# Two linear-attention and MLP layers on one core: x loads, the order of a key's split, deferred queries' phi, and the plan of the first MLP block

## The chip, the core and the metric

The kernel runs on one core of a Trainium2 chip. The metric is the device time of one execution in microseconds (us). Engines are named as in the profile: PE is the matrix engine (TensorE), DVE is VectorE, ACT is ScalarE, POOL is GpSimd, SP is the engine whose queue issues all DMAs here. Each engine takes its instructions strictly in the order in which the kernel writes them.

## The reference

x is 2048 x 448 in fp32. A layer of linear attention (16 heads of 28) and an MLP (448 to 1792 to 448) are applied twice, with the same weights:

```python
def _A_ref(x, wqkv, wo):
    q, k, v = ...                                   # (x @ wqkv), 16 heads
    phi = lambda t: jnp.where(t > 0, t + 1, jnp.exp(t)) + 1e-6
    pq, pk = phi(q), phi(k)
    kv = jnp.einsum("bhsd,bhse->bhde", pk, v)
    z = jnp.einsum("bhsd->bhd", pk)
    num = jnp.einsum("bhqd,bhde->bhqe", pq, kv)
    den = jnp.einsum("bhqd,bhd->bhq", pq, z)[..., None] + 1e-6
    return (num / den) @ wo                          # heads joined again
def _B_ref(x, w1, b1, w2, b2):
    return gelu(x @ w1 + b1) @ w2 + b2               # tanh form
x = x + _A_ref(_layernorm(x), A_wqkv, A_wo)
x = x + _B_ref(_layernorm(x), B_w1, B_b1, B_w2, B_b2)
x = x + _A_ref(_layernorm(x), A_wqkv, A_wo)
x = x + _B_ref(_layernorm(x), B_w1, B_b1, B_w2, B_b2)
```

## The kernel before

x is cut into 16 tiles of 128 rows; four tiles make a block. fp32 products are made of three matmuls on rounded halves: a value is split into hi (a copy in the format fp32r) and lo (the value minus hi), and hi·hi, hi·lo and lo·hi are added up. Most work off PE is this splitting: ACT writes hi, DVE or POOL subtracts for lo.

A layer has three stages.

**Phase 1** (`phase1`, L474) takes a tile per step t. Tokens of a string say what a step writes, in order (`STEP` L458; the first step of each layer has its own, `STEP_0` L459): `a` statistics of the tiles that `NORM[l][t]` names (one or two, ahead of t; `ln_stats` L179: bn_stats, bn_aggr, an add on DVE, a pow on POOL), `n` their normalisation (L359 on DVE; for early tiles a copy of the last 64 columns, `tail` L363, on ACT), `T` and `X` the transposed x of tile t+1 split into XH and XL (for the first tiles of layer 0 on PE into a PSUM bank, L232; later tiles by DVE's 32x32 transposes, `tu`/`tv` L255, a store to DRAM L261 and a load that spreads it, L267, token `sp`), `K` the product for k (psk), `kp` its phi (two ACT passes L293 and L294, one DVE instruction L296), `kh` its split into kh (ACT, L411) and kl (DVE, L412) and the running sum za, `s` the split of x into xnh (ACT) and xnl (POOL), `G` the sum over the previous tile of x times phi(k) in four PSUM banks, `Q` the product for q (psq) and `qp` its phi, stored to pq_d in DRAM (L430); `bg` brings in and splits pieces of w1 and w2. v is never made: G is multiplied by v's weights afterwards. Loads of x (`load_x` L80, nine buffers) are asked for at the start of each step up to one tile past the ones that the next step normalises (L480).

PSUM has eight banks: tag "m" has two (k, and later transposes), "h" two (q, transposed x in layer 0, later the MLP's hidden hp), "acc" four. Work buffers have tags too; "e" has three and holds phi's intermediate results and later the MLP's g.

**Between the phases**, `ORDER` (L450) writes out by hand what happens for the first block: `Q` and `Qp` for the last queries, deferred from phase 1, `z` and `gt` (z and G copied to SBUF), `kv`, `mask`, `m`/`ms` (the combined matrix M and its split), `qz`/`qs` (the denominator's product on POOL and `q_scale` L616 on DVE), `tq`/`qq` (q transposed and split), `o` (q times M), `la` (added to x, statistics), `lb` (`o_n` L675: normalisation, and the last 64 columns a second time by L196, then b2 added to x by POOL, L678), `T`/`x` (transposed and split for the MLP).

**The MLP** takes four blocks of four tiles. For each of its 14 slices of the hidden width, `mlp1` (L705) makes hp, ACT's GELU g (L717), gh (L720) and gl (DVE, L721); `mlp2` (L724) adds g times w2 into four banks y, and the last slice adds y to x on DVE (L735) and stores it. Behind the slices of a block, `behind` (L786) prepares the next one, step by step, by a plan: `PLAN_0` (L743) for block 0, `PLAN_1` and `PLAN` after. Its tokens: `ld` load pq, `z` and `p` the denominator, q_scale and DVE's transposes of a later block's queries, `sq`/`lq` store and spread them, `q`, `o`, `n` as above, `sx`/`lx` store and spread the normalised x, `x` split it, `g` load x. From step 7 on `z`, `p`, `sq` and `lq` serve the block after next.

Of the kernel before, what the change touches and what calls it, by code (L numbers as in the profile page):

```python
# [22 lines left out]
def linear_attn_mlp_kernel(  # L23
# [47 lines left out]
    def t512(tag, bufs, name, dt=F32):  # L71
        return work.tile([128, 512], dt, name=name, tag=tag, bufs=bufs)
# [114 lines left out]
        pool.tensor_tensor(rs, ve, mhalf, op=OP.pow)  # L187
        return xs, mv, rs

    def ln_norm(stats, name, twice=True):  # L190

        xs, mv, rs = stats
        xn = t512("xn", 2, name)
        dve.tensor_scalar(xn[:, :D], xs, mv[:, 0:1], rs, op0=OP.subtract, op1=OP.mult)  # L194
        if twice:
            dve.tensor_scalar(xn[:, D:], xs[:, TL:], mv[:, 0:1], rs, op0=OP.subtract, op1=OP.mult)  # L196
        return xn


# [25 lines left out]

    tps = {}

    def transpose_x(xn, key, j, tail=None, tag="m"):
        block(key)
        tp = tps[key, j] = bank(tag, 2, "tp")  # L230
        for c in range(4):
            pe.transpose(tp[:, c * 128:(c + 1) * 128],  # L232
                         tail if tail is not None and c == 3 else xn[:, c * 128:(c + 1) * 128], ident)

    def split_x(key, j):
        tp = tps.pop((key, j))
# [138 lines left out]

    def stage_b(l, t):
        if t < TURNED[l]:
            transpose_x(xns[l, t], ("a", l, t // 4), t % 4, tails.pop((l, t)), "h")

    def stage_x(l, t):  # L380
        key = ("a", l, t // 4)
# [22 lines left out]

    ke = {}

    def stage_kh(l, t, za):
        e = ke.pop((l, t))
        kh = t512("E", 2, "kh", F32R)[:, :D]
        kl = t512("F", 2, "kl", F32R)[:, :D]  # L410
        act.activation(kh, e, AF.Identity, bias=tiny)  # L411
        dve.scalar_tensor_tensor(kl, e, 1e-6, f(kh), op0=OP.add, op1=OP.subtract)  # L412
        if t == 0:
            dve.tensor_copy(za, e)
        else:
            dve.tensor_tensor(za, e, za, op=OP.add)
        ks[l, t] = (kh, kl)
# [3 lines left out]
    def stage_q(l, t):  # L421
        if t is None:
            return
        qo.append((l, t, proj("q", ("a", l, t // 4), t % 4)))

    def stage_qphi():
        while qo:
            l, t, o = qo.pop(0)
            e = phi(o, "eq")
            sp.dma_start(pq_d[l][t * 128:(t + 1) * 128, :], e)  # L430

    def stage_g(l, t, acc):
        h, lo = split.pop((l, t))
        kh, kl = ks.pop((l, t))
        first, last = t == 0, t == NT - 1
        for c in range(3):
            s = slice(c * 128, (c + 1) * 128)
            pe.matmul(acc[c], h[:, s], kh, start=first, stop=False)  # L438
            pe.matmul(acc[c], h[:, s], kl, start=False, stop=False)  # L439
            pe.matmul(acc[c], lo[:, s], kh, start=False, stop=last)  # L440
        pe.matmul(acc[3], h[:, TL:], kh, start=first, stop=False)
        pe.matmul(acc[3], h[:, TL:], kl, start=False, stop=last)
# [5 lines left out]


    ORDER = (  # L450
# [4 lines left out]
    )  # L455
    DEFER = NT - ORDER.split().count("Q")

    STEP = "a qp K T X s n G kp tu kh tv bg Q sp"  # L458
    STEP_0 = "K T X w a kp n s kh tu tv G Q bg sp", "K T X s kp a kh n tu tv G Q bg sp"  # L459
    NORM = (  # L460
        ((2,), (3, 4), (5, 6), (7,), (8,), (9,), (10, 11), (12,), (13, 14), (15,)),
        ((5,), (6,), (7,), (8,), (9, 10), (11,), (12,), (13, 14), (15,)),
# [11 lines left out]
    def phase1(l, tr):  # L474
        za = consts.tile([128, D], F32, name="za", tag="za")
        acc = [bank("acc", 4, f"G{c}")[:, :D] for c in range(4)]
        for t in range(NT):
            norm = NORM[l][t] if t < len(NORM[l]) else ()
            if t + 1 < len(NORM[l]):
                load_to(l, min(NORM[l][t + 1][-1] + 1, NT - 1))  # L480
            for tok in (STEP if t else STEP_0[l]).split():
                if tok == "sp":
                    for u in norm:
                        if u % 2:
                            stage_sp(l, u)
                elif tok == "a":
                    for u in norm:
                        stage_a(l, u)
                elif tok == "n":
                    for u in norm:  # L490
                        stage_n(l, u)
                elif tok == "tu":
                    for u in norm[:1]:
                        stage_t(l, u)
                elif tok == "tv":
                    for u in norm[1:]:
                        stage_t(l, u)
                elif tok == "w":
                    split_hi("q", 3, st_q)
                    split_lo("q", 3, st_q, dve)  # L500
                elif tok == "T" and t + 1 < NT:
                    stage_b(l, t + 1)
                elif tok == "X" and t + 1 < NT and (l == 0 or t + 1 >= 4):
                    stage_x(l, t + 1)
                elif tok == "K":
                    stage_k(l, t)
                elif tok == "qp":
                    stage_qphi()
                elif tok == "kp":
                    stage_kphi(l, t)  # L510
                elif tok == "kh":
                    stage_kh(l, t, za)
                elif tok == "s":
                    stage_s(l, t)
                elif tok == "G" and t >= 1:
                    stage_g(l, t - 1, acc)
                elif tok == "bg" and l == 0:
                    background(BG[t])
                elif tok == "Q" and t < DEFER:
                    stage_q(l, t)  # L520
            if l == 0 and t == 4:
                sp.dma_start(b1s, b1.rearrange("(c p) -> p c", p=128))
                sp.dma_start(b2b, b2[None, :].to_broadcast([128, D]))
            if t == 11:
                tr.wv = stage_square(wqkv[:, 2 * D:])
            if t == 13:
                trans_load(l, tr)
        return za, acc
# [19 lines left out]
    def trans_gt(tr, acc):  # L548
        tr.gt = []
        for c in range(4):  # L550
            s = t512("A" if c < 2 else "B", 2, "gt")[:, :D]
            if c % 2 == 0:
                act.copy(s, acc[c])
            else:
                dve.tensor_copy(s, acc[c])
            tr.gt.append(s)

    def trans_kv(tr):
# [115 lines left out]

    def o_n(l, b, j):  # L675
        t = b * 4 + j
        xns["m", l, t] = ln_norm(sts.pop(("m", l, t)), f"xm{l}_{t}", b == 0)
        pool.tensor_tensor(xt[l, t], xt[l, t], b2b, op=OP.add)  # L678

    def m_transpose(l, b, j):  # L680
        transpose_x(xns.pop(("m", l, b * 4 + j)), ("m", l, b), j)

    def m_split(l, b, j):
        split_x(("m", l, b), j)
# [39 lines left out]
    def mlp2(l, b, i, acc):  # L724
# [23 lines left out]
        "q0 lq1",  # L748
        "q1 o0",
        "o1 n0 q2 ld0",  # L750
        "o2 n1 sx0 q3",
        "o3 n2 lx0 ld1",
        "n3 sx1 ld2",
        "x0 lx1 ld3 z0",
        "x1 p0 z1",
        "x2 x3 p1 sq0 z2",
        "p2 z3 lq0",
    )
    LATER = (
        "n3 sx1 ld1 ld2",  # L760
# [82 lines left out]
    for l in range(LAYERS):  # L843
# [6 lines left out]
        def pre(j):  # L850
# [2 lines left out]
            q_z(l, 1, 0, tr)  # L853

        tok_ = SimpleNamespace(
            Q=lambda j: stage_q(l, fill.pop(0)), Qp=lambda j: stage_qphi(), G=lambda j: stage_g(l, NT - 1, acc),
            ld=lambda j: (load_pq(l, 0, j), load_x(l, j)), z=lambda j: trans_z(tr, za), gt=lambda j: trans_gt(tr, acc),
            kv=lambda j: trans_kv(tr), mask=lambda j: trans_mask(tr), m=lambda j: trans_m(tr, j),
            ms=lambda j: trans_ms(tr, j), qz=lambda j: q_z(l, 0, j, tr), qs=lambda j: q_scale(l, 0, j, tr),
# [10 lines left out]
        for b in range(NB):  # L870
            acc = [bank("acc", 4, f"y{j}")[:, :D] for j in range(4)]
            nxt = b + 1 < NB
            if not nxt and l + 1 < LAYERS:
                st_k = stage_square(wqkv[:, D:2 * D])
                st_q = stage_square(wqkv[:, :D])
                load_to(l + 1, PRE - 1)
            for i in range(NF):
                if i + 1 < NF:
                    mlp1(l, b, i + 1)
                elif nxt:  # L880
                    mlp1(l, b + 1, 0)
                if l == 0 and b == 0:
                    background(1 if i else 2, 0 if not i else 1)
                if nxt:
                    behind(l, b, i, tr)
                elif l + 1 < LAYERS:
                    if i == 2:
                        split_kq("k", st_k)
                    if i == 5:
                        split_kq("q", st_q)  # L890
                    if i in (3, 4, 6, 7, 8):
                        t = (3, 4, 6, 7, 8).index(i)
                        stage_a(l + 1, t)
                        stage_n(l + 1, t)
                        stage_t(l + 1, t)
                        if t % 2:
                            stage_sp(l + 1, t)
                    if 9 <= i < 13:
                        stage_x(l + 1, i - 9)
                mlp2(l, b, i, acc)  # L900
# [28 lines left out]
```

## Time and profile before

| | us |
|---|---|
| median of three runs | 896.62 (896.31 to 897.45) |
| the profiled execution, its own time | 895.62 |
| its span, first to last instruction | 893.9 |

| engine and what it waited for | idle time before that group of instructions, us |
|---|---|
| DVE, for gh (L721) | 307.3 |
| ACT, for hp (L717) | 403.4 |
| POOL, for the sum before the pow (L187) | 304.8 |

PE's granted clock is at full speed in all 40 slices of the page; DMA engines are busy 5 to 7 tenths of the time in the first eighth of the span, and mostly 1 to 5 later. A line of a timeline has: start, duration, engine, line of the kernel, operation, what it writes <- what it reads, how many, and in brackets the idle time before and what ended it. "SPq" is SP's queue of DMA issues, with the time that SP spent on them, not the transfer. Matmuls overlap their neighbours, so a matmul of 0.36 us is followed by the next after 0.20 us.

In layer 0, phase 1 runs from 6.9 to about 115 us, the work between the phases until 147.8 us, when the first hp matmul starts. Layer 1's phase 1 has its first G matmul at 460.02 us.

### The profile page before, as it was taken

To read this page: it belongs to the slowest core of one execution; us is meant where nothing else is said; L and a number is where in the kernel's file an instruction comes from. 1 tells how busy PE (TensorE), PEld (TensorE's weight loads), DVE (VectorE), ACT (ScalarE), POOL (GpSimd) and SP (SyncE) were. 2 spreads that over 40 slices of the span, in tenths; PEclk is the share of its full clock that TensorE was granted. 3 is DMA by queue.
4 is the path that set the end of the run, shared out by engine and by line. 5 is a ranking of instruction groups with operands and counts; after the bars stand their busy time and mean duration, and the time that the engine had idled before them with its cause. 6 is when DMAs were issued, how large, how long until landed. Compare 5 with 4: busy or idle time off the path is not lost.

```text
span 893.9 us, 11662 instructions
## 1 busy us (share of the span) xinstructions
PE 879.7 (98%) x4190; PEld 771.8 (86%) x4190; DVE 498.3 (56%) x968; ACT 338.3 (38%) x582; POOL 209.1 (23%) x241
## 2 busy tenths in 40 slices
PE   8999999999999999999999999999999999999998
PEld 6898978888788888888889998888878888888887
DVE  6787686655754544225469866864565473532112
ACT  5666744333222322333345564343132233223221
POOL 4566723422112012002023332320311210210000
PEclk9999999999999999999999999999999999999999
DMA  5486622723513412051145542053233323111001
GB/s 164 138 231 217 200 85 89 224 64 102 171 51 91 141 36 77 18 176 48 47 138 178 181 122 94 21 178 113 71 103 129 97 86 130 37 59 37 4 1 42
DMA packets 62761, 93.70 MB, mean 105 GB/s; under 512 B 8816, under 2 KB 57968, under 8 KB 62704
## 3 DMA queue, kind: packets, MB, share of 16 engines
q1 hardware_dynamic: 62704, 92.97, 32.9%
q8 instruction: 33, 0.54, 0.3%
q14 instruction: 24, 0.20, 0.1%
HBM read 55.65 MB, written 34.08 MB: 100 GB/s over the span
## 4 chain that ended last, share of the span: by engine, by line
PE 85%; DVE 8%; ACT 2%; DMA 2%; issue 2%; SPq 1%; POOL 1%; DVEq 0%; POOLq 0%
PE y L729 10%; PE y L731 10%; PE y L730 10%; PE hp L713 9%; PE hp L712 9%; PE hp L711 9%; PE hp L715 3%; PE hp L714 3%; PE G L439 2%; PE op L664 2%; PE op L663 2%; PE op L665 2%; PE G L440 2%; PE G L438 2%; PE psk L283 2%
## 5 line engine op out<-in xcount | busy, mean ns | idle before, releaser
L721 DVE TENSOR_TENSOR gl<-g,gh 128x512 fp32r<-128x512 f32 x112 | 79.5, 710 | 307.3 <-ACT gh L720 307.3
L717 ACT ACTIVATE g<-hp,b1s 128x512 f32<-128x512 f32 x112 | 77.1, 688 | 403.4 <-PE hp L715 403.2
L729 PE MATMUL y<-w2h,gh 128*128 128x448 f32 x448 | 163.8, 366 | 1.7 <-ACT g L717 1.7
L731 PE MATMUL y<-w2h,gl 128*128 128x448 f32 x448 | 163.7, 365 | 0.0
L730 PE MATMUL y<-w2l,gh 128*128 128x448 f32 x448 | 163.6, 365 | 0.0
L713 PE MATMUL hp<-XL,w1h 128*128 128x512 f32 x336 | 131.3, 391 | 0.3 <-DVE XL L274 0.3
L711 PE MATMUL hp<-XH,w1h 128*128 128x512 f32 x336 | 131.5, 391 | 0.1
L712 PE MATMUL hp<-XH,w1l 128*128 128x512 f32 x336 | 131.6, 392 | 0.0
L187 POOL TENSOR_TENSOR brs<-bve,mhalf 128x1 f32<-128x1 f32 x64 | 39.7, 620 | 304.8 <-DVE bve L185 302.0
L729 PEld LDWEIGHTS y<-w2h,gh 128*128 128x128 f32 x448 | 84.1, 188 | 11.4 <-ACT g L717 2.5
L730 PEld LDWEIGHTS y<-w2l,gh 128*128 128x128 f32 x448 | 84.1, 188 | 8.3
L731 PEld LDWEIGHTS y<-w2h,gl 128*128 128x128 f32 x448 | 84.2, 188 | 6.7
L713 PEld LDWEIGHTS hp<-XL,w1h 128*128 128x128 f32 x336 | 63.1, 188 | 14.8 <-DVE XL L274 1.2
L711 PEld LDWEIGHTS hp<-XH,w1h 128*128 128x128 f32 x336 | 63.1, 188 | 11.7 <-ACT XH L273 0.8
L712 PEld LDWEIGHTS hp<-XH,w1l 128*128 128x128 f32 x336 | 63.1, 188 | 11.2
L720 ACT CAST gh<-g 128x512 fp32r<-128x512 f32 x112 | 69.7, 622 | 3.6
L614 POOL TENSOR_TENSOR pz<-pq,zb 128x448 f32<-128x448 f32 x32 | 36.7, 1149 | 105.3 <-DVE dn L620 74.4
L392 POOL TENSOR_TENSOR xnl<-x,xnh 128x384 fp32r<-128x384 f32 x32 | 37.4, 1168 | 45.2 <-ACT xnh L391 20.4
L181 DVE BATCH_NORM_STATS2 bst<-x 128x6 f32<-128x448 f32 x64 | 39.7, 621 | 10.0 <-DMA x<-in_A_x_dram 7.4
L678 POOL TENSOR_TENSOR x<-x,b2b 128x448 f32<-128x448 f32 x32 | 36.9, 1152 | 31.5 <-DVE xm L194 23.3
L715 PE MATMUL hp<-XL,w1x 128*128 128x512 f32 x112 | 43.6, 389 | 0.0
L714 PE MATMUL hp<-XH,w1x 128*128 128x512 f32 x112 | 43.6, 389 | 0.0
(140 smaller groups left out, 1571.4 us busy)
## 6 DMA issues: line engine op xcount, KB each, us to landing
x<-in_A_x_dram SPq DMA_DIRECT2D x32, 224.0 KB, 4.2
pq_d<-eq SPq DMA_DIRECT2D x32, 224.0 KB, 2.1
pq<-pq_d SPq DMA_DIRECT2D x32, 224.0 KB, 3.3
x<-x_d SPq DMA_DIRECT2D x32, 224.0 KB, 3.6
sq_a<-sq SPq DMA_DIRECT2D x13, 512.0 KB, 2.6
sp<-sq_a SPq DMA_DIRECT2D x52, 128.0 KB, 3.0
sq_q<-sq SPq DMA_DIRECT2D x12, 512.0 KB, 2.8
sp<-sq_q SPq DMA_DIRECT2D x48, 128.0 KB, 3.0
```

The lines of the kernel that those rows point to most:

```text
L181: dve.bn_stats(st, xs)
L711: pe.matmul(o, w1h[:, c, s], x.moving(x.hi, c), start=(c == 0), stop=False)
L712: pe.matmul(o, w1l[:, c, s], x.moving(x.hi, c), start=False, stop=False)
L713: pe.matmul(o, w1h[:, c, s], x.moving(x.lo, c), start=False, stop=False)
L714: pe.matmul(o, w1x[:, s], x.moving(x.hi, 3), start=False, stop=False)
L715: pe.matmul(o, w1x[:, s], x.moving(x.lo, 3), start=False, stop=True)
L717: act.activation(g, hp, AF.Gelu_apprx_tanh, bias=b1s[:, i:i + 1])
L720: act.copy(gh, g)
L721: dve.tensor_sub(gl, g, f(gh))
L729: pe.matmul(acc[j], gh[:, s], w2h[:, i], start=first, stop=False)
L730: pe.matmul(acc[j], gh[:, s], w2l[:, i], start=False, stop=False)
L731: pe.matmul(acc[j], gl[:, s], w2h[:, i], start=False, stop=last)
```

## The change

- `stage_kh` is cut in two: `stage_kh` (ACT) and `stage_kl` (DVE, za). In `STEP_0` kh is written ahead of the next tile's norm and split (layer 0) and kl has a place of its own; layer 1's first step has `n` ahead of `kl`. A new `STEP_1` serves steps 1 to 3 of layer 0, with `qp`, `K`, `T`, `X` ahead of `a`.
- Loads of x are asked for at the end of a step (`ld`, ahead of `sp`), up to the tiles that the step after next normalises.
- The six deferred queries get `fill_qphi`: exp and both relus on ACT, the add on POOL, two "e" buffers, one query for each `Qp`; `ORDER` is rewritten, with the third `Q` ahead of `tq0`.
- gt's four copies are all on ACT; the second copy of xm's last columns moves from DVE (L196) to ACT; the adds of b2 move out of `o_n` into the first four steps of each MLP block (`add_bias`).
- In `PLAN_0` p0, p1 and p2 of the block after next come one or two steps earlier, and x2 and x3 one step earlier; the last step is empty.

```diff
-    def stage_kh(l, t, za):
+    def stage_kh(l, t):
+        kh = t512("E", 2, "kh", F32R)[:, :D]
+        act.activation(kh, ke[l, t], AF.Identity, bias=tiny)
+        ks[l, t] = (kh,)
+
+    def stage_kl(l, t, za):
         e = ke.pop((l, t))
-        kh = t512("E", 2, "kh", F32R)[:, :D]
+        kh, = ks[l, t]
         kl = t512("F", 2, "kl", F32R)[:, :D]
-        act.activation(kh, e, AF.Identity, bias=tiny)
         dve.scalar_tensor_tensor(kl, e, 1e-6, f(kh), op0=OP.add, op1=OP.subtract)
...
+    def fill_qphi():
+
+        l, t, o = qo.pop(0)
+        e = t512("e", 3, "eq")[:, :D]
+        p = t512("e", 3, "ep")[:, :D]
+        act.activation(e, o, AF.Relu, scale=-1.0)
+        act.activation(e, e, AF.Exp, scale=-1.0)
+        act.activation(p, o, AF.Relu)
+        pool.tensor_tensor(e, p, e, op=OP.add)
+        sp.dma_start(pq_d[l][t * 128:(t + 1) * 128, :], e)
...
     ORDER = (
-        "Q ld1 z ld0 ld2 qz0 qz1 G gt qs1 Qp Q kv qs0 tq1 mask qz2 tq0 qs2 ld3 "
-        "m0 qq1 m1 qz3 ms0 qs3 m2 ms2 m3 ms1 qq0 ms3 Q tq2 Qp o0 la0 tq3 qq2 qq3 "
-        "lb0 o1 o2 la1 T0 la2 o3 Q lb1 lb2 x0 la3 Qp T1 x1 T2 Q lb3 Qp x2 "
-        "T3 x3 Q Qp pre "
+        "Q ld1 z ld0 ld2 qz0 qz1 G gt qs1 Q Qp kv qs0 tq1 Q mask qz2 tq0 qs2 ld3 "
+        "m0 qq1 Qp m1 qz3 ms0 qq0 m2 ms1 m3 ms2 tq2 ms3 qs3 o0 Qp la0 tq3 qq2 qq3 "
+        "o1 lb0 o2 la1 T0 la2 o3 Q lb1 x0 lb2 T1 la3 T2 x1 Q Qp lb3 x2 "
+        "T3 x3 Q Qp Qp pre "
     )
-    STEP = "a qp K T X s n G kp tu kh tv bg Q sp"
-    STEP_0 = "K T X w a kp n s kh tu tv G Q bg sp", "K T X s kp a kh n tu tv G Q bg sp"
+    STEP = "a qp K T X s n G kp kh tu kl tv bg Q ld sp"
+    STEP_0 = "K T X w a kp kh n kl s Q bg ld sp", "K T X s kp a kh n kl tu Q ld sp"
+    STEP_1 = "qp K T X a s n G kp kh tu kl tv bg Q ld sp"
...
-            if t + 1 < len(NORM[l]):
-                load_to(l, min(NORM[l][t + 1][-1] + 1, NT - 1))
-            for tok in (STEP if t else STEP_0[l]).split():
+            if t == 0:
+                load_to(l, NORM[l][1][-1])
+            for tok in (STEP_0[l] if t == 0 else STEP_1 if l == 0 and t < 4 else STEP).split():
...
+                elif tok == "ld" and t + 2 < len(NORM[l]):
+                    load_to(l, NORM[l][t + 2][-1])
...
-            if c % 2 == 0:
-                act.copy(s, acc[c])
-            else:
-                dve.tensor_copy(s, acc[c])
+            act.copy(s, acc[c])
...
     def o_n(l, b, j):
         t = b * 4 + j
-        xns["m", l, t] = ln_norm(sts.pop(("m", l, t)), f"xm{l}_{t}", b == 0)
+        xn = xns["m", l, t] = ln_norm(sts.pop(("m", l, t)), f"xm{l}_{t}")
+        if b == 0:
+            act.copy(xn[:, D:], xn[:, TL:D])
+
+    def add_bias(l, b, j):
+        t = b * 4 + j
         pool.tensor_tensor(xt[l, t], xt[l, t], b2b, op=OP.add)
...
-        "o2 n1 sx0 q3",
-        "o3 n2 lx0 ld1",
-        "n3 sx1 ld2",
-        "x0 lx1 ld3 z0",
-        "x1 p0 z1",
-        "x2 x3 p1 sq0 z2",
+        "o2 n1 sx0 q3 ld1",
+        "o3 n2 lx0 ld2 z0",
+        "n3 sx1 ld3 p0 z1",
+        "x0 lx1 p1 z2 sq0",
+        "x1 x2 x3",
         "p2 z3 lq0",
+        "",
```

More of the change, by code (lines that the diff above doesn't have):

```diff
@@ L188, in ln_stats, with ln_norm @@
         return xs, mv, rs
-    def ln_norm(stats, name, twice=True):
+    def ln_norm(stats, name):
         xs, mv, rs = stats
@@ L194, in ln_norm @@
         dve.tensor_scalar(xn[:, :D], xs, mv[:, 0:1], rs, op0=OP.subtract, op1=OP.mult)
-        if twice:
-            dve.tensor_scalar(xn[:, D:], xs[:, TL:], mv[:, 0:1], rs, op0=OP.subtract, op1=OP.mult)
         return xn
@@ L226, in linear_attn_mlp_kernel, with transpose_x @@
     tps = {}
-    def transpose_x(xn, key, j, tail=None, tag="m"):
+    def transpose_x(xn, tail, key, j, tag="m"):
         block(key)
@@ L231, in transpose_x @@
         for c in range(4):
-            pe.transpose(tp[:, c * 128:(c + 1) * 128],
-                         tail if tail is not None and c == 3 else xn[:, c * 128:(c + 1) * 128], ident)
+            pe.transpose(tp[:, c * 128:(c + 1) * 128], xn[:, c * 128:(c + 1) * 128] if c < 3 else tail, ident)
     def split_x(key, j):
@@ L377, in stage_b @@
         if t < TURNED[l]:
-            transpose_x(xns[l, t], ("a", l, t // 4), t % 4, tails.pop((l, t)), "h")
+            transpose_x(xns[l, t], tails.pop((l, t)), ("a", l, t // 4), t % 4, "h")
     def stage_x(l, t):
@@ L511, in phase1 @@
                 elif tok == "kh":
-                    stage_kh(l, t, za)
+                    stage_kh(l, t)
+                elif tok == "kl":
+                    stage_kl(l, t, za)
                 elif tok == "s":
@@ L676, in o_n @@
         t = b * 4 + j
-        xns["m", l, t] = ln_norm(sts.pop(("m", l, t)), f"xm{l}_{t}", b == 0)
+        xn = xns["m", l, t] = ln_norm(sts.pop(("m", l, t)), f"xm{l}_{t}")
[3 more added lines that the diff above has]
+        t = b * 4 + j
         pool.tensor_tensor(xt[l, t], xt[l, t], b2b, op=OP.add)
     def m_transpose(l, b, j):
-        transpose_x(xns.pop(("m", l, b * 4 + j)), ("m", l, b), j)
+        xn = xns.pop(("m", l, b * 4 + j))
+        transpose_x(xn, xn[:, TL:], ("m", l, b), j)
     def m_split(l, b, j):
@@ L855, in linear_attn_mlp_kernel @@
         tok_ = SimpleNamespace(
-            Q=lambda j: stage_q(l, fill.pop(0)), Qp=lambda j: stage_qphi(), G=lambda j: stage_g(l, NT - 1, acc),
+            Q=lambda j: stage_q(l, fill.pop(0)), Qp=lambda j: fill_qphi(), G=lambda j: stage_g(l, NT - 1, acc),
             ld=lambda j: (load_pq(l, 0, j), load_x(l, j)), z=lambda j: trans_z(tr, za), gt=lambda j: trans_gt(tr, acc),
@@ L883, in linear_attn_mlp_kernel @@
                     background(1 if i else 2, 0 if not i else 1)
+                if i < 4:
+                    add_bias(l, b, i)
                 if nxt:
```

## The prediction

> **What bounds the kernel now.** I read the page's busy shares, then the list of what PE waited for, then the timelines of the engines around each of those waits.
>
> ```profile
> PE 879.7 (98%) x4190; PEld 771.8 (86%) x4190; DVE 498.3 (56%) x968; ACT 338.3 (38%) x582; POOL 209.1 (23%) x241
> ```
>
> PE sets the span: only 893.9 - 879.7 = 14.2 us have no matmul in them, and the change takes no matmul away. All that it can win lies in PE's waits:
>
> ```profile
> PE y L729 <- ACT g L717: 1.7, 2, 0.9
> PE psq L283 <- DVE eq L296: 1.3, 2, 0.6
> ...
> PE tq L632 <- DVE kvm L567: 1.1, 2, 0.5
> PE G L438 <- ACT kh L411: 1.0, 2, 0.7
> ...
> PE tp L232 <- DVE xm L194: 0.6, 2, 0.3
> PE op L654 <- DVE ql L642: 0.6, 2, 0.4
> ```
>
> Columns: total, times, longest. A wait costs more than its idle time, since neighbouring matmuls overlap:
>
> ```profile
> 76.32 0.37 PE L287 MATMUL psk<-wk,XL 128*128 128x448 f32 x1
> 77.34 0.47 PE L438 MATMUL G<-kh,xnh 128*128 128x448 f32 x1 [0.66 <-ACT kh L411]
> ```
>
> Starts are 0.20 apart when nothing waits, here 1.02: 0.66 idle cost 0.82, and the next start came 0.1 late as well. I count this way, start to start. What kept PE waiting stands on VectorE and on SP's DMA queue:
>
> ```profile
> 20.05 0.62 DVE L181 BATCH_NORM_STATS2 bst<-x 128x6 f32<-128x448 f32 x1
> ...
> 20.99 0.61 DVE L296 SCALAR_TENSOR_TENSOR eq<-psq,eq 128x448 f32<-128x448 f32 x1
> ...
> 72.35 0.63 DVE L181 BATCH_NORM_STATS2 bst<-x 128x6 f32<-128x448 f32 x1 [2.08 <-DMA x<-in_A_x_dram]
> ...
> 139.64 1.33 DVE L194 TENSOR_SCALAR xm<-x,bmv,brs 128x448 f32<-128x448 f32 x1 [0.22 <-POOL brs L187]
> ...
> 231.88 0.27 DVE L256 STREAM_TRANSPOSE sq<-pq 128x128 f32<-128x128 f32 x1
> 232.07 2.18 DVE L735 TENSOR_TENSOR x<-y,x 128x448 f32<-128x448 f32 x4
> ...
> 459.71 0.61 DVE L412 SCALAR_TENSOR_TENSOR kl<-psk,kh 128x448 fp32r<-128x448 f32 x1
> 460.24 0.61 DVE L414 COPY za<-psk 128x448 f32<-128x448 f32 x1
> 460.77 0.50 DVE L359 TENSOR_SCALAR x<-x,bmv,brs 128x448 f32<-128x448 f32 x1
> ```
> ```profile
> 66.76 1.75 SPq L267 DMA_DIRECT2D sp<-sq_a  x4
> 68.55 0.90 SPq L82 DMA_DIRECT2D x<-in_A_x_dram  x2
> ```
>
> **(a) kh first, qp first: layer 0, steps 0 to 3: -1.1.** phi of k ends at 15.97, yet kh ran at 17.38, behind L363 and L391. Moved, it runs 16.0-16.65; kl follows x_2's norm (ends 16.67) at 16.7 instead of 18.04. G's third matmul then waits only for GpSimd's xnl (17.5-18.55): 18.6 instead of 19.02, -0.4. The next Q waited for eq at 20.99, which stood behind two tiles' statistics (1.9); with qp first eq runs at 18.5 and Q starts at 20.45, not 21.66. What is late next is VectorE's own chain: kl, za, eq, XL, statistics, then a pow on GpSimd (0.55 and two hand-overs, once hidden by eq and XL, now bare), norm, tail, ek, kh, kl. It puts step 1's kl at 26.4 (was 26.80 at its end), so G there is only 0.4 early; step 2's G is 1.0 early, step 3's Q 1.1. Later steps wait for nothing. Bounds: -0.3 (the chain eats all but G's 0.4) to -1.6 (all three eq and both first kh waits gone).
>
> **(b) x loads: -2.3.** Not more look-ahead: each step now asks for one tile less, at the step's end, ahead of the spread (L267), which waits on SP for its store to land. x_14 was issued behind it at 68.55 and reached VectorE at 72.35; now x_13 and x_14 go out behind the w1 pieces at about 66.3 and, at the same 3.8, land by 70.1. With (a) everything on SP is 1.1 earlier too. VectorE gets some 2 us back, so PE's waits at 73.84 (0.65), 76.32 (0.82) and 77.34 (0.56), and at 89.26 (0.38, ScalarE still catching up), go: -2.4, of which I keep 2.3. x_11 likewise passes b1s and b2b (before: 2.55 idle at 54.4). Paid for it: x_8 (37.9, was 23), x_10 (50.4, was 45.1) and x_13 (66.3, was 61.25) are issued later, just before need. Bounds: -0.4 (one of these becomes the late one) to -2.8.
>
> **(c) Between the phases, twice: -1.35 each.** Waits before, layer 0: tq0 for the mask 0.70, o0 for ql 0.70, T2 0.43, T3 0.55. Third Q now stands between tq1 and tq0 and covers the mask (2.2 against 0.7). gt: four copies on ScalarE (0.54); the second needs the slot that G frees at 115.26, and the other two and the first phi queue behind it; they end at 116.75, under the Q that ends at 117.4: nothing. Each deferred phi: VectorE loses 0.55, ScalarE does three passes (0.55 + 0.58 + 0.55 = 1.7), GpSimd an add (1.15, as L678); the store follows the add. L196 (0.31) becomes a ScalarE copy (0.30, as L363), one hand-over later; the b2b adds move into the first MLP steps, where GpSimd idles for 8.0. The order by adding these rows along PE: kv to 120.36, tq1 0.36, Q 2.26, tq0 0.37, four mp 3.0, tq2 0.45: o0 at 126.8 (was 127.58), its ql ready at 126.05, so without its wait. Then tq3 waits, and o1 behind it, for q_scale 3, which now follows ms3 on VectorE (last Ml to 127.7, four steps of 0.61 + 0.18 + 0.25 + 0.62: 129.5, or 130.0 beside an add; PE free 129.3): +0.5; T1 and T2 run without wait, T3 about on time; the first hp waits for the fifth phi's third pass (bank "h"), 146.4 against 146.2: +0.3. First hp at 146.5 instead of 147.84. Then ScalarE has one phi left (1.7, then the 1.28 table load): g is ready 0.2 before y needs it. Bounds: -2.2 (no new wait) to +0.8 (see the second rival).
>
> The row on ports: L194 takes 0.50, but 1.33 at 139.64, while GpSimd's add of b2b ran 139.57-140.72. The Trainium skill, page "SBUF — State Buffer", section "Who interferes with whom", says VectorE and GpSimd share a port pair as an exclusive lock: a VectorE instruction in a two-port mode or with two SBUF inputs blocks while GpSimd reads, and the other way round. By that rule, on which the trace agrees, (c) would shrink where an add meets such an instruction.
>
> **(d) Block 0's plan, twice: -1.85 each.** y's first matmul of block 1 (231.56 to 232.80: 1.02 + 0.08 late) is named after g, but g had been done; it needed y's banks, which L735 frees, and L735 stood behind q_scale and turn of p2 until 232.07. p2 is now a step earlier: 1.1 gone. x2 and x3 move from step 12 to 11: the XH and XL waits (0.33 + 0.43) go; their spread was issued 212.82-214.56, lands by 217.6 (median 3.0 after the issue), ScalarE comes at 218.2. VectorE's step 9 holds gl 0.7, n3 1.4, p0 3.1 = 5.2 against PE's 4.95, with 2.9 of slack in gl. Bounds: -1.9 to -1.0 (the spread late).
>
> **(e) w2 pieces late, layer 0: +0.6.** The last pq store comes 0.5 later behind hp's start, so the pq loads, the 14 pieces of M and w2 behind them on SP do too; before, ScalarE's g (164.87) already waited for w2, and gl ended at 167.87, 0.27 before its matmul. Bounds: 0 to 1.2.
>
> **(f) Layer 1, step 0: +1.3.** There n is ahead of kl now: L359 waits for the pow (459.94 + 0.55), runs 460.5-461.0, kl 461.05-461.67, where G's second matmul took it at 460.38. Nothing covers it. kh gains nothing there. Bounds: +1.0 to +1.4.
>
> Sum: -1.1 - 2.3 - 2.7 - 3.7 + 0.6 + 1.3 = -7.9. The profiled run took 895.62 (span 893.9 and 1.7 around it), so 887.7; the median shown is 1.0 above that run: **888.7**.
>
> **Rivals.**
> 1. *x is late elsewhere* (b is -0.4): 890.6. For it: 223 to 233 GB/s in 40-80 us and only 3 us between issue and need. Against: these tiles pass the spread. 0.15.
> 2. *GpSimd's adds hold VectorE up between the phases*: four of the six adds fall where VectorE scales pq or normalises xm; at 1.33 - 0.50 = 0.83 each, less 1.2 of slack, 2.1 more per layer: (c) at +0.75, 892.9. Against: VectorE loses twelve instructions there (six eq, two gt, four L196). 0.17. This is the case in which the port rule decides.
> 3. *No new wait* (c -2.2, e 0, a -1.6): 885.9. 0.13.
> 4. *Slower*: tag "e" has 3 buffers; each phi now holds two, until add and store have landed, and g needs one too. If the stores took so long that the last two phis and g ran one after the other, each wait 3.5 per layer: -5.2 for the rest, +7 here: 898.4. It decides from a landing of some 6 us; pq_d's stores show a median of 2.1. 0.04.
>
> My forecast has 0.48 and 886.8-890.4 as its own range; 0.03 is left for no change (rivals 1 and 2 together with the low ends). About 0.2%, 1.8 us, can be told from no change here. Faster 0.93, same 0.03, slower 0.04. Range 885.4 to 892.9.
>
> **What would show it.** After: eq no longer among PE's releasers; L181 without a DMA wait near 70; first hp about 1.3 earlier against G; no idle at y's first matmul of block 1; G L439 in layer 1 waiting 1.1 to 1.3 for kl; a new wait of tq3. Wrong if PE waits for x, for "e" or for w2 by more than 1 us.

## The result and the profile after

The changed kernel took 893.16 us (median of five runs, 891.85 to 893.72) beside 896.62 for the kernel before (five runs): ratio 0.9957, 95% interval 0.9942 to 0.9971. Measured again later (e13 below) the ratio was 0.9953 (0.9939 to 0.9966). So it is faster by 0.4 to 0.5%, 3.5 to 4.9 us by the medians, where 7.9 were forecast and 3.7 was the least that the range allowed. The profiled run took 892.87 (span 891.2), 2.75 less than the profiled run before.

The first part of the page and the list of what PE waited for, of the changed kernel (total, times, longest):

```profile
PE 876.6 (98%) x4190; PEld 770.7 (86%) x4190; DVE 488.9 (55%) x944; ACT 346.1 (39%) x606; POOL 225.8 (25%) x253
```
```profile
PE tq L646 <- PE op L668: 2.0, 2, 1.0
PE G L451 <- DVE kl L413: 1.8, 4, 1.2
PE tp L230 <- DVE x L356: 1.6, 2, 1.1
PE G L450 <- ACT kh L406: 1.4, 2, 0.9
...
PE y L751 <- DVE gl L741: 0.6, 1, 0.6
PE y L749 <- ACT gh L740: 0.6, 2, 0.3
```

The waits that the change was to remove are gone: eq, kvm and ql are no longer among PE's releasers, and neither is g at y's first matmul. Others stand in their place: tq twice, kl and kh, gh and gl. PE's busy time is no measure here: it fell from 879.7 to 876.6 us though the same 4190 matmuls run.

Where the time went, by when the same matmul starts in the two traces (after minus before, us; zp is the small product with which the work between the phases begins, the second hp the group behind y's first matmuls): zp of layer 0 +0.12, the first hp -0.81, the second hp +0.15, block 1's first o +1.37 and its first y -0.43, then -0.57 at layer 1's first G, +0.64 at the next psq, -1.03 at zp, -1.75 at the first hp, -0.75 at the second, -2.50 at block 1's first y. So block 0's plan gained 1.8 in each layer, step 0 of layer 1 lost 1.2, what the stages between the phases gained was gone one hp later, layer 0's phase 1 gained nothing, and from psq to zp in layer 1 1.67 us came in that no step of the forecast had.

### The profile page after: what moved, and what is told of

Same layout as the page of the kernel before. It is cut to its first block, busy times and chain, and to the rows that moved or that the text cites. A ratio compares the mean times of both kernels' runs of the same rounds, so it can differ in the third digit from the quotient of the medians.

```text
span 891.2 us, 11669 instructions
## 1 busy us (share of the span) xinstructions
PE 876.6 (98%) x4190; PEld 770.7 (86%) x4190; DVE 488.9 (55%) x944; ACT 346.1 (39%) x606; POOL 225.8 (25%) x253
## 4 chain that ended last, share of the span: by engine, by line
PE 88%; DVE 5%; ACT 3%; DMA 2%; POOL 1%; issue 1%; SPq 1%; POOLq 0%; ACTq 0%; DVEq 0%
PE y L751 10%; PE y L749 10%; PE y L750 10%; PE hp L731 8%; PE hp L732 8%; PE hp L733 8%; PE hp L735 3%; PE hp L734 3%; PE G L451 2%; PE G L452 2%; PE op L678 2%; PE G L450 2%; PE op L677 2%; PE op L679 2%; PE psq L282 2%; PE psq L280 2%
## 5 line engine op out<-in xcount | busy, mean ns | idle before, releaser
L271 DVE TENSOR_TENSOR XL<-sp,XH 128x512 fp32r<-128x512 f32 x50 | 41.7, 840 | 4.0 <-ACT XH L270 4.0
```

The source lines that it names most:

```text
L271: dve.tensor_sub(lo.rearrange("p (c i n) -> p c i n", c=4, n=32), x, f(h))
```

## The experiments

The runs came in groups, each group on one chip with the kernel before beside it: e1 to e4 (before 895.19), e5 to e8 (894.89), e9 to e12 and e13 to e15 (one chip, 896.45 and 897.15). Ratios are to that. "PE's waits" are the starts' distances above the usual one for that pair of instructions, those over 0.06 us, summed over a stretch of the trace.

**e1: block 0's plan alone**, on the kernel before.

```diff
-    PLAN_0 = (... "n3 sx1 ld2", "x0 lx1 ld3 z0", "x1 p0 z1", "x2 x3 p1 sq0 z2", "p2 z3 lq0",
+    PLAN_0 = (... "n3 sx1 ld3 p0 z1", "x0 lx1 p1 z2 sq0", "x1 x2 x3", "p2 z3 lq0", "",
```

> The kernel before with nothing of the change but block 0's new plan. Theory: the plan's two shifts act by themselves, 1.85 us per layer: 3.7 us faster than before, about 892.9, and so as fast as the whole change; PE's waits ahead of y's first matmul of block 1 and for XH and XL of tiles 2 and 3 gone in both layers, every landmark up to there as in before. Rival: half of it needs the work between the phases to be out of the way first: 1.8 us faster at most.

891.03 us, ratio 0.9960 (0.9948 to 0.9972): 3.6 us, as much as the whole change. In its trace y's first matmul of block 1 starts 1.80 and 1.78 us earlier against block 1's first o; 1.85 was forecast. The changed kernel's trace shows the place, VectorE's adds of y to x in block 0's last slice (at 232.07 in before) and y's first matmul of block 1 on PE:

```profile
229.62 2.21 DVE L755 TENSOR_TENSOR x<-y,x 128x448 f32<-128x448 f32 x4
...
232.15 0.39 PE L735 MATMUL hp<-XL,w1x 128*128 128x512 f32 x1
232.37 0.36 PE L749 MATMUL y<-w2h,gh 128*128 128x448 f32 x1
```

It is 0.22 from start to start, where 1.24 stood. All the other edits together come to nothing, and the question is which of them gain and which lose.

**e7 and e12: the loads of x.** e7 is the changed kernel with the old rule, e12 the kernel before with the new one.

```diff
-            if t == 0:
-                load_to(l, NORM[l][1][-1])
+            if t + 1 < len(NORM[l]):
+                load_to(l, min(NORM[l][t + 1][-1] + 1, NT - 1))
...
-                elif tok == "ld" and t + 2 < len(NORM[l]):
-                    load_to(l, NORM[l][t + 2][-1])
```

> The changed kernel with x loaded by the rule of before (at the start of each step, one tile more). Theory: the new rule gained nothing here, since VectorE comes to these tiles as late as before for another reason: within 0.3 us of the changed kernel, with DMA waits of VectorE at about 56 us (2.5 us) and 72 us back and PE's waits between 69 and 78 us about as they are. Rival: the rule gains what was forecast: 1.9 to 2.8 us slower than the changed kernel.

> The kernel before with the new rule of loading x alone (two steps ahead, at the step's end ahead of the spread). Theory: the rule acts by itself, as its removal from the changed kernel cost some 3 us: VectorE's DMA waits at 54 and 72 us go, and PE's waits between 69 and 90 us (2.4 us) with them: 1.5 to 2.5 us faster than before. Rival: it works only where the phi and kh come early: within 0.7 us of before.

e7: 893.70, ratio 0.9992 (0.9980 to 1.0003). Without the new rule the changed kernel's gain is gone; set against 0.9953 to 0.9957 the rule is worth 3.1 to 3.5 us. e12: 893.51, ratio 0.9972 (0.9961 to 0.9983): 2.5 us by itself. The theory behind e7's expectation, drawn from one trace of the changed kernel, fell; the size that the forecast gave (b) stands. What had misled is VectorE's timeline, the first three lines of the changed kernel, the last of e7:

```profile
69.93 0.61 DVE L417 TENSOR_TENSOR za<-psk,za 128x448 f32<-128x448 f32 x1
70.97 0.63 DVE L181 BATCH_NORM_STATS2 bst<-x 128x6 f32<-128x448 f32 x1 [0.42 <-DMA x<-in_A_x_dram]
...
72.33 0.63 DVE L181 BATCH_NORM_STATS2 bst<-x 128x6 f32<-128x448 f32 x1 [0.33 <-DMA x<-in_A_x_dram]
```
```profile
72.77 0.63 DVE L181 BATCH_NORM_STATS2 bst<-x 128x6 f32<-128x448 f32 x1 [1.75 <-DMA x<-in_A_x_dram]
```

The DMA waits shrank from 2.08 to 0.42 and 0.33, but VectorE itself came late, so the second statistics ran at 72.33, as before at 72.35. And one profile says little here: PE's waits from 60 to 80 us are 2.1 in this one, but 0.6, 0.8, 1.0, 1.0, 1.1, 1.1 and 2.5 in seven others of the same instructions up to there (e2, e3, e10, e13, e4, e8, e9); with the old rule they are 3.2 (e7), and 2.2 and 2.1 in before and e1. Neither one-part trace shows the size that the times show: e12's profiled run was the slowest of its eleven (896.46) and e7's the fastest of its twelve (893.11).

**e5 and e6: the order of steps 1 to 3 in layer 0.** e5 drops `STEP_1`, so that the next tiles' statistics stand ahead of the deferred phi again; kh first stays. e6 puts them right behind the phi.

```diff
-            for tok in (STEP_0[l] if t == 0 else STEP_1 if l == 0 and t < 4 else STEP).split():
+            for tok in (STEP_0[l] if t == 0 else STEP).split():
```
```diff
-    STEP_1 = "qp K T X a s n G kp kh tu kl tv bg Q ld sp"
+    STEP_1 = "qp a K T X s n G kp kh tu kl tv bg Q ld sp"
```

> The changed kernel with statistics ahead of the deferred phi in layer 0's steps 1 to 3, as in before (kh ahead of kl and the loads stay). Theory: with the phi first, the statistics' pow on GpSimd lies bare on VectorE's chain and the norm collides with xnl, which made phi of step 3, w1's pieces and the spreads 1.7 us late and kept PE's waits at 69 to 78 us; undone, eq's waits of 0.5 to 1.1 us come back in steps 2 and 3, and 1.5 to 2 us of waits between 69 and 78 us go: 0.3 to 1.0 us faster than the changed kernel. Rival: the waits between 69 and 78 us come from the x loads themselves: they stay, and eq's waits come on top: 1.0 to 1.6 us slower.

> The changed kernel with the statistics right behind the deferred phi and ahead of XL's eviction in steps 1 to 3 of layer 0, so that the pow lies under XL. Theory: VectorE's idle 0.44, 0.44 and 0.73 us for the pow goes, phi of step 3 is 1.0 to 1.7 us earlier, and G's waits at 26.8 and the ones from 69 to 78 us shrink: 0.8 to 1.6 us faster than the changed kernel. Rival: XL, 1.5 us later, is what phase 1 then waits for: 0.5 us slower or more.

e5: 889.42, ratio 0.9943 (0.9927 to 0.9958), some 1 us better than the changed kernel; the intervals overlap, so the size rests on the traces. PE's waits from 20 to 95 us: before 5.1, the changed kernel's order 3.3 to 5.6 (eight traces), e5 1.5, with none from 42 to 95 us. Later runs with e5's order (e11, e14, e15) have 1.4 to 2.1. The start of zp, where layer 0's phase 1 ends, says the same: against before it lies at -1.6 to +0.45 in the eight traces (mean -0.7), at -2.2, -4.0, -3.4 and -2.9 in these four (mean -3.1). So the phi's place takes back some 2.4 us. VectorE and GpSimd of the changed kernel in step 1 of layer 0, then VectorE of e5:

```profile
20.92 0.62 DVE L181 BATCH_NORM_STATS2 bst<-x 128x6 f32<-128x448 f32 x1
...
22.81 1.21 DVE L356 TENSOR_SCALAR x<-x,bmv,brs 128x448 f32<-128x448 f32 x1 [0.44 <-POOL brs L187]
25.43 0.63 DVE L293 SCALAR_TENSOR_TENSOR psk<-psk,ek 128x448 f32<-128x448 f32 x1 [1.42 <-ACT ek L291]
26.77 0.62 DVE L413 SCALAR_TENSOR_TENSOR kl<-psk,kh 128x448 fp32r<-128x448 f32 x1 [0.70 <-ACT kh L406]
...
22.09 0.68 POOL L187 TENSOR_TENSOR brs<-bve,mhalf 128x1 f32<-128x1 f32 x1 [0.39 <-DVE bve L185]
22.74 1.02 POOL L389 TENSOR_TENSOR xnl<-x,xnh 128x384 fp32r<-128x384 f32 x1
```
```profile
20.90 0.68 DVE L236 TENSOR_TENSOR XL<-tp,XH 128x512 fp32r<-128x512 f32 x1
21.50 1.31 DVE L356 TENSOR_SCALAR x<-x,bmv,brs 128x448 f32<-128x448 f32 x2
24.23 0.63 DVE L293 SCALAR_TENSOR_TENSOR psk<-psk,ek 128x448 f32<-128x448 f32 x1 [1.42 <-ACT ek L291]
25.57 0.62 DVE L413 SCALAR_TENSOR_TENSOR kl<-psk,kh 128x448 fp32r<-128x448 f32 x1 [0.70 <-ACT kh L406]
```

With the phi first, nothing lies between the second statistics and its norm: VectorE waits 0.44 for the pow, and the norm, alone 0.51 (21.86 in the same trace), takes 1.21 beside GpSimd's xnl. Two norms end at 24.0 there and at 22.8 in e5, and ek, phi, kh and kl follow in one chain. PE then waits 1.14 for kh and 0.46 for kl, the same to 0.02 in five profiles of this order; in e5 both are under 0.1, and eq, whose waits come back (0.81 and 0.20), costs less. The delay goes on: phi of step 3 runs at 40.22 (before 38.50), w1's pieces on GpSimd 1.7 later, so their buffers, SP's next loads of w1 and the spreads are 1.5 to 2.2 later, and XL of tile 6 keeps VectorE idle for 1.84 at 52. e6 took the 0.44 away (kl at 26.17) and gained nothing that shows: 891.74, ratio 0.9961 (0.9948 to 0.9974).

**e9 and e4: tq3.** e9 moves the third deferred phi behind tq3; e4 moves z 3 ahead of the second phi's add and q_scale 3 ahead of Ml 1 to 3.

```diff
-        "... ms3 qs3 o0 Qp la0 tq3 qq2 qq3 "  "o1 lb0 ..."
+        "... ms3 qs3 o0 la0 tq3 qq2 qq3 "  "Qp o1 lb0 ..."
```
```diff
-        "m0 qq1 Qp m1 qz3 ms0 qq0 m2 ms1 m3 ms2 tq2 ms3 qs3 o0 Qp la0 tq3 qq2 qq3 "
+        "m0 qq1 qz3 Qp m1 ms0 qq0 qs3 m2 ms1 m3 ms2 tq2 ms3 o0 Qp la0 tq3 qq2 qq3 "
```

> The changed kernel with the third deferred phi moved behind tq3 and its splits, so that GpSimd's add (129.0 to 130.1) no longer runs beside q_scale 3's last operation (L639, 1.47 us there). Theory (the port): L639 falls to about 0.62 us, q_scale 3 is done 0.85 us earlier, and PE's wait at tq3 falls from 1.14 to 0.2-0.4 us in both layers: 1.5 us faster than the changed kernel. Rival: L639 is long, or q_scale 3 late, for another reason: the wait stays at 1.1 and the time as it is.

> The changed kernel with z 3 ahead of the second deferred phi's add on GpSimd and q_scale 3 ahead of the last three evictions of M on VectorE. Theory: tq3's wait (1.14 us in each layer) goes, since q_scale 3 is done 3 us earlier and away from GpSimd's add; 0.9 us per layer reach the first hp: 1.8 us faster, about 891.1. Rival: q_scale 3 now holds Ml up, and the first o waits for it, or the first hp waits for the fifth phi instead: 0.0 to 0.6 us.

e9: 890.07, ratio 0.9926 (0.9913 to 0.9939), 2.2 us below the changed kernel on that chip (892.28). The changed kernel's timeline of VectorE, GpSimd and PE at tq3 in layer 0, then VectorE of e9:

```profile
129.15 1.47 DVE L639 SCALAR_TENSOR_TENSOR pq<-pq,rd 128x448 f32<-128x448 f32 x1
...
129.00 1.14 POOL L441 TENSOR_TENSOR eq<-ep,eq 128x448 f32<-128x448 f32 x1 [3.43 <-ACT ep L440]
...
130.72 0.62 PE L646 MATMUL tq<-ident,pq 128*112 128x128 f32 x4 [0.98 <-PE op L668]
```
```profile
129.35 0.62 DVE L639 SCALAR_TENSOR_TENSOR pq<-pq,rd 128x448 f32<-128x448 f32 x1
```

The same instruction takes 1.47 beside the add and 0.62 without it, and PE's wait at tq3 fell from 1.14 to 0.26 and 0.29. (The page names the last o as releaser of tq; that had ended, and L639 is what came last.) The Trainium skill, page "SBUF — State Buffer", section "Who interferes with whom", has VectorE and GpSimd exclude each other on a shared port pair; this pair of lines and the norm beside xnl agree. e4: 891.09, ratio 0.9955 (0.9942 to 0.9968), no difference by time. Its rival came: L639 took 0.63 and tq3 did not wait, but the first o waited 0.75 for Ml, which stood behind q_scale 3.

**e2: the GELU's table.** One GELU of 128x1 behind the last deferred phi.

```diff
+        act.activation(junk, tiny, AF.Gelu_apprx_tanh)
         mlp1(l, 0, 0)
```

> The changed kernel with a GELU of 128x1 on ScalarE behind the last deferred phi, so that the table is loaded then. Theory: in the changed kernel the table load carries the GELU's wait for hp and starts only when hp is done; with the load ahead of it g is ready 1.1 us earlier, and the four PE waits around y's first matmuls (0.44, 0.10, 0.22, 0.10) go in both layers: 1.5 to 1.7 us faster than the changed kernel, about 891.3. Rival: GELU waits for a buffer of tag e, which GpSimd's add and the store of the last phi free late, and the load is no matter: 0.0 to 0.3 us.

890.63, ratio 0.9953 (0.9941 to 0.9965): no difference by time. ScalarE ahead of the first g in before; then the same and PE's first y in the changed kernel; then ScalarE in e2:

```profile
148.61 0.58 ACT L294 ACTIVATE eq<-eq 128x448 f32<-128x448 f32 x1
149.21 1.28 ACT L717 ACT_TABLE_LOAD   x1
150.58 0.69 ACT L717 ACTIVATE g<-hp,b1s 128x512 f32<-128x512 f32 x1
```
```profile
148.24 0.55 ACT L440 ACTIVATE ep<-psq 128x448 f32<-128x448 f32 x1
149.90 1.28 ACT L737 ACT_TABLE_LOAD   x1 [1.11 <-PE hp L735]
151.20 0.69 ACT L737 ACTIVATE g<-hp,b1s 128x512 f32<-128x512 f32 x1
...
152.59 0.47 PE L749 MATMUL y<-w2h,gh 128*128 128x448 f32 x1 [0.28 <-ACT gh L740]
```
```profile
146.78 0.55 ACT L441 ACTIVATE ep<-psq 128x448 f32<-128x448 f32 x1
147.35 1.28 ACT L889 ACT_TABLE_LOAD   x1
148.64 0.20 ACT L889 ACTIVATE junk<-tiny 128x1 f32<-128x1 f32 x1
148.75 0.67 ACT L738 ACTIVATE g<-hp,b1s 128x512 f32<-128x512 f32 x1
```

Nothing but the GELU needs hp, yet in the changed kernel the load waits for it: in the compiled order the GELU has two waits there, for hp and, since the buffers of tag "e" are now freed by GpSimd's add, for that; the load carries the first of them. In before the load ran at once behind the last exp, under hp (from 147.84), and so it does in e10 below, without the add. With the table early, the four waits at y (0.44, 0.10, 0.22, 0.10) go in layer 0 and half of them in layer 1. In layer 0 part of the gain is given back: PE waits 1.95 from 160 to 180 us instead of 1.23 (1.66 in e13), since w2's pieces land at their own time.

**e8: w2's late pieces**, taken in one MLP step later.

```diff
-                if l == 0 and b == 0:
+                if l == 0 and b == 0 and i != 1:
                     background(1 if i else 2, 0 if not i else 1)
```

> The changed kernel with the late pieces of w2 taken in by ScalarE from the third MLP step of layer 0's block 0 on, not from the second. Theory: g of step 1 and 2 waits on ScalarE behind w2's piece; PE's waits at y (0.79 and 0.10 us at 168, 0.23 and 0.10 at 174) go: 1.0 to 1.2 us faster than the changed kernel. Rival: the pieces, one step later, meet the spread and the evictions of block 1, and half comes back: 0.3 to 0.6 us.

891.05, ratio 0.9965 (0.9954 to 0.9977): not faster by time. In the trace PE's waits from 160 to 180 us went from 1.23 (1.66 in e13) to none. ScalarE in the changed kernel, then in e8:

```profile
165.52 0.57 ACT L325 CAST w2h<-stg 128x448 fp32r<-128x448 f32 x1 [6.01 <-DMA stg<-in_B_w_dram]
166.00 0.68 ACT L737 ACTIVATE g<-hp,b1s 128x512 f32<-128x512 f32 x1
```
```profile
162.63 0.69 ACT L737 ACTIVATE g<-hp,b1s 128x512 f32<-128x512 f32 x1 [3.60 <-PE hp L735]
...
165.25 0.57 ACT L325 CAST w2h<-stg 128x448 fp32r<-128x448 f32 x1 [1.27 <-DMA stg<-in_B_w_dram]
```

In the one g stands behind w2's piece, in the other ahead of it. e8's profiled execution lost 1.67 in layer 1's phase 1 by the pace (below), more than such a gain; whether its other nine executions did is not known.

**e10 and e15: the deferred phi's last pass back on VectorE**, in the changed kernel (e10) and with the five mends of e11 (e15).

```diff
-        act.activation(e, o, AF.Relu, scale=-1.0)
-        act.activation(e, e, AF.Exp, scale=-1.0)
-        act.activation(p, o, AF.Relu)
-        pool.tensor_tensor(e, p, e, op=OP.add)
+        e = phi(o, "eq")
```

> The changed kernel with the deferred phi's last pass back on VectorE (max and add in one operation, no third pass on ScalarE, no add on GpSimd), all else as in the change. Theory: handing phi to ScalarE and GpSimd is worth nothing here: no add runs beside L639, so tq3 waits 0.3 to 0.6 us, not 1.14; the table load no longer stands behind the GELU's wait for hp, so g is ready in time and y's first matmuls do not wait (0.85 us); VectorE's 0.55 us per phi costs less than 0.5 us per layer: 0.5 to 2 us faster than the changed kernel. Rival: VectorE is what these stages lack: the waits for the mask and for the transposes of T2 and T3 come back (0.7 to 1.5 us per layer): 0.5 to 1.5 us slower.

> The five mends, and the deferred phi's last pass back on VectorE. Theory: with the add away from q_scale 3 and the table loaded early, phi's place is worth little: PE waits for the fifth phi at the first hp (0.3) and for a transpose (0.4) in each layer: 0.5 to 1.5 us slower than the five mends. Rival: what made phi back on VectorE 1.4 us faster than the changed kernel with the third phi moved is more than these two waits: 1 us faster or more.

e10: 889.61, ratio 0.9918 (0.9906 to 0.9930), 2.7 below the changed kernel. tq3's wait is 0.26 and 0.29, y's waits are gone in both layers, and a transpose (0.39) and the first hp (0.32, for eq) wait instead. So in the change as written, handing phi over costs more than it brings. e15: 887.87, ratio 0.9905 (0.9891 to 0.9918), 3.2 slower than e11 (884.64), more than forecast: once the third phi and the table have their places, ScalarE and GpSimd doing it is worth 2.0 of that. So much shows between the phases: from zp to the second hp e11 is 1.75 and 1.18 us shorter than before, e15 0.55 and 0.34. The rest lies in layer 0's phase 1, where both have the same instructions.

**e3 and e14: kl ahead of the norm in layer 1's step 0.** e3 does it in the changed kernel; e14 is e11 without it.

```diff
-    STEP_0 = ..., "K T X s kp a kh n kl tu Q ld sp"
+    STEP_0 = ..., "K T X s kp a kh kl n tu Q ld sp"
```

> The changed kernel with kl ahead of the norm in layer 1's step 0, as in before. Theory: PE's wait of 1.40 us for kl at 459 us goes: 1.3 us faster, about 891.6. Rival: the matmuls' pace of layer 1's phase 1 (starts 202.7 ns apart in the changed kernel, 206.7 ns in before, from about 461 us on) hangs on that long wait: then the slow pace is back, 1.7 us are lost, and the kernel is 0.3 us slower than the changed one.

> The five mends without one: kl stays behind the norm in layer 1's step 0. Theory: PE's wait of 1.4 us is back and 1.25 us are lost against the five mends (about 0.9867 + 0.0014 of before). Rival: the pace: after the long wait the matmuls of layer 1's phase 1 started 202.7 ns apart in eight traces of nine, after the short one 206.7 ns in four of five; if the long wait brings the quick pace, 1.7 us come back, and the kernel is 0.3 to 0.5 us faster than the five mends.

e3: 890.08, ratio 0.9951 (0.9938 to 0.9965), no difference by time, though in its trace the wait fell from 1.40 to 0.16 and the matmuls kept the quick pace, 202.7 ns. e14: 884.83, ratio 0.9868 (0.9852 to 0.9885), the same as e11, though its wait of 1.40 is back. e14's trace bears out its rival, 1.22 lost and 1.67 gained back; the 0.3 to 0.5 us between them do not show in the times. PE of the changed kernel, whose step is e14's too, then PE of e11:

```profile
459.45 0.36 PE L450 MATMUL G<-kh,xnh 128*128 128x448 f32 x1
461.05 0.47 PE L451 MATMUL G<-kl,xnh 128*128 128x448 f32 x1 [1.24 <-DVE kl L413]
461.36 0.36 PE L452 MATMUL G<-kh,xnl 128*128 128x448 f32 x1
461.56 0.36 PE L450 MATMUL G<-kh,xnh 128*128 128x448 f32 x1
461.76 0.37 PE L451 MATMUL G<-kl,xnh 128*128 128x448 f32 x1
461.97 0.36 PE L452 MATMUL G<-kh,xnl 128*128 128x448 f32 x1
```
```profile
452.33 0.36 PE L451 MATMUL G<-kh,xnh 128*128 128x448 f32 x1
452.69 0.47 PE L452 MATMUL G<-kl,xnh 128*128 128x448 f32 x1
...
453.21 0.37 PE L451 MATMUL G<-kh,xnh 128*128 128x448 f32 x1
453.42 0.37 PE L452 MATMUL G<-kl,xnh 128*128 128x448 f32 x1
453.62 0.37 PE L453 MATMUL G<-kh,xnl 128*128 128x448 f32 x1
453.83 0.37 PE L451 MATMUL G<-kh,xnh 128*128 128x448 f32 x1
```

Behind the long wait the starts are 0.203 apart on average, behind the short one 0.207, and so on for some 85 us, 400 matmuls, with nothing waiting: e11 is 1.76 us ahead of e14 at the next psq and 0.09 at zp. The table by stretches shows it at the same granted clock; e11, then e14 (us, PE, PEld, DVE, ACT, POOL busy, clock, DMA share, GB/s):

```profile
480.00:500.00 20.00, 20.00 (x99) 18.16 (x98) 18.27 (x39) 11.13 (x21) 6.56 (x10) 1.00 0.55 175
```
```profile
480.00:500.00 20.00, 20.00 (x101) 18.53 (x100) 18.62 (x39) 11.51 (x22) 6.73 (x10) 1.00 0.58 186
```

**e13 and e11: the changed kernel again, and five mends together** (e5, e3, e2, e9 and e8; phi stays on ScalarE and GpSimd).

> The changed kernel itself, beside the two below and the kernel before on one chip, with a second profile. If its median lies 3 to 4 us below before, as in the first measurement, then the one-part runs can be set against that; if it lies 5 us or more below, part of what they seemed to gain was the chip's. Its PE waits from 60 to 80 us tell whether 2.1 us in the first trace was typical: the unchanged stretches of other runs had 0.6 to 1.1.

> The changed kernel with five mends together: statistics ahead of the deferred phi in steps 1 to 3, kl ahead of the norm in layer 1's step 0, the GELU table loaded ahead of hp, the third deferred phi behind tq3, the late pieces of w2 one step later. Theory: the terms add, 1.8 + 1.25 + 1.5 + 1.5 + 1.0 us by PE's waits in the traces: 6 to 7 us faster than the changed kernel, ratio to before 0.988 to 0.990. Rival: the gains in layer 0 run into each other ahead of w2's pieces and the chunks of M, which come by DMA at their own time: 3.5 to 4.5 us, ratio 0.991 to 0.992.

e13: 892.28, ratio 0.9953 (0.9939 to 0.9966). e11: 884.64, ratio 0.9867 (0.9854 to 0.9879): 7.6 us below e13 and 1.3% below the kernel before, more than forecast for it, though hardly a single mend but e9 showed clearly by time. Its page:

```profile
PE 875.0 (99%) x4190; PEld 772.0 (87%) x4190; DVE 486.5 (55%) x944; ACT 346.5 (39%) x608; POOL 225.2 (26%) x253
```

## Why the forecast was right in sign and half the size

| step | forecast | measured | from |
|---|---|---|---|
| (a) kh first, phi first | -1.1 | 0 to +1.4 | e5: kh first -1.0 (waits at 20 to 40 us, 1.4 for before's 2.3); the phi's place +1.0 by time (intervals overlap), +2.4 by the start of zp |
| (b) loads of x | -2.3 | -2.5 (-1.5 to -3.5) | e12, by time; -3.1 to -3.5 by e7 |
| (c) between the phases, both layers | -2.7 | +0.3 | starts of zp and of the second hp |
| (d) block 0's plan, both layers | -3.7 | -3.6 (-2.5 to -4.7) | e1 |
| (e) w2's pieces | +0.6 | +0.8 to +1.7 | eight traces against before's (1.2 in the first); none in e8 |
| (f) kl behind the norm | +1.3 | +1.2 | traces of both |
| pace behind it | not in it | -1.7 | traces of both, e14 against e11 |

With the middle of each, the measured column sums to about -4.4; the runs gave -3.5 to -4.9. The rows of (a) and (b) are the loosest: together they make -1.8, the eight traces up to zp -0.7.

(d) and (f) held as worked out: the place, the mechanism and the size. (b) held in its size, by time. Its place shows only with the phi back in before's place: there (e5, e11, e14, e15, all with kh first) PE's waits from 42 to 95 us, 2.7 and 2.6 in before and e1, are at most 0.7. In the changed kernel they are 1.3 to 3.4 (eight traces); x_14, put at 70.1, was still waited for at 72.33 in the first of them.

(a) failed at "What is late next is VectorE's own chain". The chain was named, with the pow bare and the tail copy in it, but mis-sized: step 1's kl was put at 26.4 and ended at 27.4. Missing was GpSimd's xnl beside the norm, 0.7 in each of steps 1 to 3; the other 0.3 was there before the moves (phi of k ended at 16.26, not 15.97). "Later steps wait for nothing" failed too: w1's pieces, SP's loads and the spreads came late with the chain. kh first was the good half: about -1 in e5.

(c) removed what it said: the mask's wait, ql's and the transposes', and the first hp came 0.93 and 0.72 earlier against zp (1.3 was forecast). The new waits were mis-sized. tq3 was put at +0.5 and cost 1.14, since the add fell on L639; both were named, "129.5, or 130.0 beside an add", and the end was 130.6. "g is ready 0.2 before y needs it" was wrong: the table load was taken to run behind the last phi, under hp, and waited for hp. That gave back 0.96 and 1.0, all of the lead. With phi left on VectorE (e10) the same stages, zp to the second hp, are 1.2 and 0.8 shorter than before, 2.0 of the 2.7 forecast. The fifth phi's wait at hp (+0.3) did not come. Rival 2 was right in kind, in one collision of its four (e9: 2.2 us for both layers); the port rule decided that term. Its time, 892.9, lies near the measured 893.16 by luck: it had (c) at +0.75 in each layer and (a) at -1.1.

(e) came to its upper end or above by before's trace, and PE waited for w2 by more than the 1 us that was to show the forecast wrong. But e1 and e12, which leave the work between the phases as in before, wait 0.5 there too, so some 0.5 of it comes without the change. Where y comes earlier (e2, e10) the wait is 2.0: the pieces land at their own time. Rival 1 fell with e7 and e12, by time. Rival 4's buffers cost no store's landing, but through them the GELU got its second wait.

"All that it can win lies in PE's waits" was wrong as well: 1.7 us were won outside them, by the pace, which no step had. That it more than made up for (f) was luck.

Not settled: which small difference in time sets the matmuls' pace; and e6's and e8's gains, which their traces show and their times do not.

## What to carry to other kernels

When work moves to engines with slack, price the place as well as the pass: the same hand-over of phi lost 2.7 us where its add met a VectorE operation and its buffers put a wait on the table load, and brought 2.0 to 3.2 once both were moved. An instruction moved to the front makes bare whatever it used to cover, here a pow and a norm, and the bill comes where that chain feeds DMAs, 20 to 50 us later. One trace can't tell a gain of 1 to 2 us that hangs on a DMA's landing; undo the edit and time both.

## What the hardware showed unexpectedly

Runs of 448-column matmuls without a wait had two paces, 202.7 and 206.7 ns from start to start, at a granted clock of 1.00. In the longest run, the 427 behind layer 1's step 0, the pace did not change in any of 17 traces; in shorter runs it also changed without a stall (once in 219 matmuls from 41.7 us in e15). In layer 1's phase 1 the pace was quick in ten of eleven traces with the 1.4 us wait in step 0 (not in e8) and in one of six with the short wait (e3). That is a link, not a cause: the e8 and e3 traces differ from their likes by a few ns around the stall.

The same instructions left PE waits of 0.6 to 2.5 us from 60 to 80 us in eight profiles. What varied with them is x's landing: VectorE waited for x between 69 and 73 us not at all in e2, e3, e10 and e13 (PE's waits 0.6 to 1.0), 0.4 and 0.7 in e4 and e8 (both 1.1), 0.75 in the changed kernel's first trace (2.1) and 1.1 in e9 (2.5).
